# Dense feed-forward: VectorE, ScalarE and SyncE also issue in program order, side work placed step by step between matmul groups, and the last batch's first two weight quarters keep their sums on chip

## The chip, the core and the metric

The kernel runs on one core of a Trainium2 chip. The metric is the device time of one execution in microseconds (us); smaller is better. Besides TensorE (PE; its weight loads are shown as PEld) the profile names VectorE (DVE), ScalarE (ACT), GpSimd (POOL) and SyncE (SP), which here only issues DMA transfers.

## What is computed

Three layers follow one another over 4 batches of 576 positions: decayed causal attention with 8 heads of 64, a feed-forward block, and a second attention with 4 experts of which two are chosen for each position. The change touches the middle one:

```python
def _moe_ref(x, U, V, w_ch1, w_ch2):           # x (4, 576, 512), w_ch1 (512, 2048)
    xt = x.transpose(0, 2, 1)
    h = xt @ U @ V
    u = x + h.transpose(0, 2, 1)
    ch = np.maximum(u @ w_ch1, 0.0) @ w_ch2     # w_ch2 (2048, 512)
    return (u + ch).astype(np.float32)
```

Every factor is split into a high and a low part, and three products (high by high, high by low, low by high) are summed in PSUM.

## The kernel before

**Steps and groups.** The 2048 hidden columns are cut into four quarters, and each batch into two halves c of 288 positions. One step is a batch, a half and a quarter: 32 steps. `ffn_stream` runs them as one generator. Step i alternates four *hidden* groups (`ffn_hidden`, L529, for step i+1: twelve matmuls into PSUM tile `hps`, then `hh` by ACT in L533 and `hl` by DVE in L534) with four *out* groups (`ffn_out`, L545, for step i: twelve matmuls into `cps`, then a DVE addition into `ust` or `yc`, L548 or L550). Both PSUM tiles come from one pool of three buffers, `psf`. Each `yield` of the stream ends one group. In the following such a group and the time it takes on PE is called a **slot**; slot 1 is the first one after the first attention has ended (402.20 us).

**Quarters 0 and 1** work in a 32-bit format (fp32r) with weights that are prepared during the first attention. Steps 0 to 15 use them: batch 3 last, first quarter 0 for both halves (steps 12 and 13), then quarter 1 for both (14 and 15). After quarter 0 its sums go to `ydram`; for quarter 1 `ffn_load` reads `ust` from `udram` again, casts it again to `uh` (L514, ACT) and `ul` (L515, POOL), and reads the sums back (L519). For batches 0 to 2 the sums stay on chip between the two quarters.

**Quarters 2 and 3** work in fp16, with scales. Steps 16 to 23 do quarter 2 and then 3 for batches 0 and 1, steps 24 to 31 for batches 2 and 3. What they need is made as *side work* beside steps 9 to 23:

- `narrow_quarter`: for each of 8 weight pieces a quarter, a 512 KB transfer into `raw` (two buffers), two ACT operations (L338, L340), two DVE operations (L341, L342, here called the joining) and a DVE maximum (L423). The next transfer into a buffer can start when the joining of the piece in it is done.
- `power`: turns a maximum into a scale over a transpose on PE (`amt`, L384), three small DVE operations on `ar` (L388 to L390), a matmul (`rsp`, L395) and two DVE operations.
- `prepare_u`: reads `ust` of a batch (576 KB for each half) and takes four DVE maxima `uam` (L465), then `power`.
- `convert_quarter` and `convert_u`: high part by ACT, low part by DVE (L448, L449 and L488, L489).

**Who orders what.** `dense_until` runs one slot of the stream, then one step of each job. But only PE was held to program order (`manual_schedule`). For DVE, ACT, SP and POOL a scheduler set the order of each queue at build time, from its own estimate of when each instruction can start. On the chip each queue is then worked off in the order that was set: an instruction that waits holds up what stands behind it on its engine.

At the end of the stretch the weights of the third layer (`wall`, `wo`) and the result of batch 0 (`load_y`) are read and split, again at places that the scheduler chose.

Of the kernel before, what the change touches and what calls it, by code (L numbers as in the profile page):

```python
# [18 lines left out]
P = 128  # L19
# [42 lines left out]
def kernel(  # L62
# [271 lines left out]
    def narrow_bytes(wt, raw):  # L334

        lo, hi = raw[:, :, 0], raw[:, :, 1]
        wi = wt.bitcast(I32)
        nc.scalar.activation(wi, raw.bitcast(U8)[:, :, 3], AF.Copy, bias=-31.0 / 64.0,  # L338
                             scale=1.0 / 32.0)
        nc.scalar.activation(f32(lo), f32(hi), AF.Copy, scale=2.0 ** -112)  # L340
        nc.vector.scalar_tensor_tensor(wi, lo, 3, wi, OP.logical_shift_left, OP.bitwise_or)  # L341
        nc.vector.scalar_tensor_tensor(wi, hi, -2147483648, wi, OP.bitwise_and, OP.bitwise_or)  # L342
# [58 lines left out]
    def narrow_quarter(w32, q):  # L401
# [34 lines left out]
    def convert_quarter(w32, q):  # L436

        w1h, w1l, w2h, w2l = W[q]
        sides = scales[q][0]
        for t in range(2 * FT):  # L440
            cs = slice(t * P, t * P + P)
            if t < FT:
                dh, dl = w1h[:, :, cs], w1l[:, :, cs]
                sv = w32[:, t, :].rearrange("p (k n) -> p k n", k=KT)
            else:
                dh, dl, sv = w2h[:, t - FT, :], w2l[:, t - FT, :], w32[:, t, :]
            up = sides[t // FT][:, 1:2]
            nc.scalar.mul(dh, sv, up)  # L448
            nc.vector.scalar_tensor_tensor(dl, sv, up, dh, OP.mult, OP.subtract)  # L449
            yield  # L450
# [23 lines left out]
    def convert_u(b, ycs):  # L474

        us, es = st_u.pop(b)
        uh = cur["fu"].tile([P, KT, S], F16, name="uhf", tag="uh")
        ul = cur["fu"].tile([P, KT, S], F16, name="ulf", tag="ul")
        for c, yc in enumerate(ycs):
            cs = slice(c * HC, c * HC + HC)  # L480
            nc.sync.dma_start(yc[:], ydram[b, :, :, cs])
            for i, step in enumerate(steps):
                if step[:2] == (b, c) and step[2] > 1:
                    loads[i] = uh[:, :, cs], ul[:, :, cs], yc, es
        for c in range(NC):
            cs = slice(c * HC, c * HC + HC)
            for k in range(0, KT, 2):
                nc.scalar.mul(uh[:, k:k + 2, cs], us[c][:, k:k + 2], es[:, 1:2])  # L488
                nc.vector.scalar_tensor_tensor(ul[:, k:k + 2, cs], us[c][:, k:k + 2], es[:, 1:2],  # L489
                                               uh[:, k:k + 2, cs], OP.mult, OP.subtract)  # L490
                yield
# [11 lines left out]
    def ffn_load(b, c, first, fy):  # L503
# [10 lines left out]
        nc.scalar.copy(uh[:], ust[:])  # L514
        nc.gpsimd.tensor_tensor(ul[:], ust[:], f32(uh[:]), OP.subtract)  # L515
        if first:
            return uh, ul, ust
        yc = fy.tile([P, KT, HC], F32, name="yc", tag="yc")
        nc.sync.dma_start(yc[:], ydram[b, :, :, cs])  # L519
        return uh, ul, yc  # L520
# [37 lines left out]
    for q in (0, 1):  # L558
        steps += [(B - 1, c, q, q == 0, True, True) for c in range(NC)]
# [7 lines left out]
    W, loads, scales = {}, {}, {}  # L567

# [9 lines left out]
    def ffn_stream():  # L578
# [8 lines left out]
        for i, (b, c, q, first, head, last) in enumerate(steps):  # L587
# [6 lines left out]
            for j in range(KT):  # L594
                if i + 1 < n:
                    q1 = steps[i + 1][2]
                    nxt.append(ffn_hidden(j, W[q1], *loads[i + 1][:2], F32R if q1 < 2 else F16))
                    yield i
                ffn_out(j, W[q], hs, yc, back)
                late = QX0 <= i + 2 < QX1  # L600
                if j == 1 and not late and (i + 2 > 4 * (B - 1) or (i + 2) % 4):
# [3 lines left out]
                if j == KT - 1 and late:  # L605
                    ffn_prepare(i + 2)
# [375 lines left out]

    more_weights(100)
    with tc.manual_schedule(engines={mybir.EngineType.PE}):
        jobs.append(in_turn(narrow_quarter(w32[2], 2), narrow_quarter(w32[3], 3)))
        jobs.append(in_turn(prepare_u(0, fy2), prepare_u(1, fy2)))
        dense_until(QX0)
        halves_of_weights()
        drain(jobs[1]) if len(jobs) > 1 else None
        del jobs[1:]  # L990
        quarters = [convert_quarter(w32[2], 2)]
        jobs.append(convert_u(0, sums_of(fy2, ("yc", "yc"))))
        while 2 not in scales:
            next(jobs[0])
        jobs.append(in_turn(*quarters))
        dense_until(QX1 - 1)
        jobs.append(convert_u(1, sums_of(fy2, ("yc", "yc"))))
        dense_until(QX1)
        drain(in_turn(*jobs))
        del jobs[:]  # L1000
        jobs.append(convert_quarter(w32[3], 3))
        dense_until(QX1 + 1)
        jobs.append(prepare_u(2, cur["fy"]))
        dense_until(QX1 + 5)
        jobs.append(in_turn(convert_u(2, sums_of(wy_pool, ("w1h", "w1l"))),
                            prepare_u(3, cur["fy"])))
# [3 lines left out]
        jobs.append(convert_u(3, sums_of(wy_pool, ("w2h", "w2l"))))  # L1010
# [16 lines left out]
    for k in range(KT):  # L1027
        for c0, c1 in ((0, 512), (512, NA)):
            st = stage.tile([P, 512], F32, name="st3", tag="wst")
            nc.sync.dma_start(st[:, 0:c1 - c0], wall[k * P:k * P + P, c0:c1])  # L1030
            nc.scalar.copy(wah[:, k, c0:c1], st[:, 0:c1 - c0])
            nc.gpsimd.tensor_tensor(wal[:, k, c0:c1], st[:, 0:c1 - c0], f32(wah[:, k, c0:c1]),
                                    OP.subtract)
    for k in range(2):
        st = stage.tile([P, 512], F32, name="st3b", tag="wst")
        nc.sync.dma_start(st[:], wo[k * P:k * P + P, :])
        nc.scalar.copy(woh[:, k, :], st[:])
        nc.gpsimd.tensor_tensor(wol[:, k, :], st[:], f32(woh[:, k, :]), OP.subtract)
# [7 lines left out]
    def load_y(b, yp, stp, tag):  # L1046
# [3 lines left out]
        nc.gpsimd.memset(f32(yl[:, :, S:SP_]), 0.0)  # L1050
        for c in range(NC):
            cs = slice(c * HC, c * HC + HC)
            st = stp.tile([P, KT, HC], F32, name="yst", tag=tag)
            nc.sync.dma_start(st[:], ydram[b, :, :, cs])
            for k in range(KT):
                nc.scalar.copy(yh[:, k, cs], st[:, k])
                nc.gpsimd.tensor_tensor(yl[:, k, cs], st[:, k], f32(yh[:, k, cs]), OP.subtract)
        return yh, yl

    y = load_y(0, sy0, fy, "yc")  # L1060
    with tc.manual_schedule(engines={mybir.EngineType.PE}):
        dense_until(len(steps))
    for p_ in (s16, fy, fh, fu, wy_pool, wx_pool, stage):
# [245 lines left out]
    with tc.manual_schedule(engines={mybir.EngineType.PE}):  # L1309
# [16 lines left out]
        one(m1)  # L1326
        with tc.issue_after(first_k):
            y_next = load_y(1, ys[1], sy, "yst")
        for h in range(NH):
# [5 lines left out]
            if e == 1 and b + 2 < B:  # L1335
                with tc.issue_after(cur["last"].ins):
                    y_next = load_y(b + 2, ys[b % 2], sy, "yst")
# [89 lines left out]
```

## Time and profile before

| | us |
|---|---|
| median of 3 runs | 894.58 |
| lowest to highest | 893.28 to 894.96 |
| profiled execution, its own time | 901.39 |
| its span from first to last instruction | 899.7 |
| mean granted TensorE clock | 0.964 of full |
| PE / DVE / ACT / POOL busy over the span | 795.6 / 608.0 / 428.8 / 282.8 |

The profiled execution is 6.8 us above the median. Shares of the whole span mix three layers with different limits; the change lies in the stretch from about 402 to 699 us, so that stretch is read by itself in the rows below.

### The profile page before, as it was taken

The page shows a single profiled execution, that of the slowest core. Times are in us where ns is not written, and L with a number is a line of the kernel's source. Part 1 is how long each engine was busy: PE and PEld are TensorE (multiplying, and loading weights), DVE is VectorE, ACT ScalarE, POOL GpSimd, SP SyncE. Part 2 cuts the span into 40 slices and gives each one's busy share as a digit, 9 for nine tenths or more (in the row PEclk, how much of TensorE's full clock was granted, in tenths as well). Part 3 has the DMA queues.
Part 4 walks back from the last instruction along what each step waited for, and adds up shares of the span by engine and source line. Part 5 has one row for each costly group of instructions (what it writes and reads, how often), then busy time and mean ns, then how long its engine had stood idle before and what let it go on. Part 6 is the DMA issues. An engine that isn't in the chain of part 4 may idle for free.

```text
span 899.7 us, 19048 instructions
## 1 busy us (share of the span) xinstructions
PE 795.6 (88%) x7412; PEld 720.2 (80%) x7412; DVE 608.0 (68%) x1598; ACT 428.8 (48%) x840; POOL 282.8 (31%) x367
## 2 busy tenths in 40 slices
PE   2588578899999999989797989999999989989997
PEld 2587477788999889989796867777777989979886
DVE  6889978975777666657778533553333678877775
ACT  3677557555545564334454311223211467665664
POOL 9856554543423442002011000007200635331210
PEclk9988789999999999999989999999999999999999
DMA  6334565543433441155566321321200530312122
GB/s 190 107 108 132 169 205 152 164 131 93 131 113 88 135 122 53 38 184 173 168 199 199 100 97 43 90 80 52 79 28 27 146 87 21 101 47 75 35 77 84
DMA packets 63146, 97.23 MB, mean 108 GB/s; under 512 B 5024, under 2 KB 43792, under 8 KB 63056
## 3 DMA queue, kind: packets, MB, share of 16 engines
q1 hardware_dynamic: 58496, 87.24, 33.1%
q10 hardware_dynamic: 4560, 8.78, 2.7%
q8 instruction: 58, 0.95, 0.5%
q14 instruction: 32, 0.26, 0.1%
HBM read 55.61 MB, written 22.56 MB: 87 GB/s over the span
## 4 chain that ended last, share of the span: by engine, by line
PE 54%; DVE 19%; DMA 14%; ACT 5%; issue 4%; POOL 3%; SPq 1%; POOLq 0%; ACTq 0%; DVEq 0%
PE cps L545 15%; PE hps L529 14%; PE sc L228 6%; DVE ph L244 4%; DMA ust<-udram 4%; DMA raw<-in_w_dram 3%; PE po L1227 3%; PE pv L1185 3%; DVE ub L185 2%; PE pq L1120 2%; PE ub L180 2%; DMA ydram<-ust 2%; PE gp L734 2%; PE av L259 1%; PE av L263 1%
## 5 line engine op out<-in xcount | busy, mean ns | idle before, releaser
L244 DVE TENSOR_TENSOR ph<-pf,ph 128x576 f16<-128x576 f32 x144 | 128.6, 898 | 31.8 <-ACT ph L243 31.1
L533 ACT ACTIVATE hh<-hps 128x288 fp32r<-128x288 f32 (+1 forms) x128 | 52.3, 409 | 203.6 <-PE hps L529 198.2
L534 DVE SCALAR_TENSOR_TENSOR hl<-hps,hh 128x288 fp32r<-128x288 f32 (+1 forms) x128 | 57.9, 453 | 88.8 <-ACT hh L533 88.4
L238 ACT ACTIVATE pf<-sc 128x576 f32<-128x576 f32 x144 | 84.3, 613 | 36.8 <-PE sc L228 32.2
L243 ACT CAST ph<-pf 128x576 f16<-128x576 f32 x144 | 89.7, 638 | 10.1 <-POOL pf L240 8.7
L228 PE MATMUL sc<-qa,ka 128*128 128x288 f32 (+4 forms) x288 | 75.8, 324 | 18.5 <-DMA qa<-mr 6.9
L185 DVE CUSTOM_DVE_ANT_0 ub<-ub,maskm 128x448 f32<-128x448 f32 x192 | 81.8, 426 | 11.5 <-PE ub L180 9.4
L545 PE MATMUL cps<-hh,w2h 128*128 128x288 f32 x256 | 81.2, 317 | 1.2 <-DVE ust L548 0.9
L545 PE MATMUL cps<-hh,w2hf 128*128 128x288 f16 x256 | 73.8, 288 | 7.4 <-DVE hl L534 7.4
L529 PE MATMUL hps<-uh,w1h 128*128 128x288 f32 x256 | 76.3, 319 | 3.7 <-DVE hl L534 2.8
L545 PE MATMUL cps<-hh,w2l 128*128 128x288 f32 x256 | 77.6, 303 | 0.0
L545 PE MATMUL cps<-hl,w2h 128*128 128x288 f32 x256 | 77.5, 303 | 0.1
L259 PE MATMUL av<-vh,ph 128*128 128x65 f16 x720 | 74.7, 199 | 2.0 <-DVE x L308 2.0
L261 PE MATMUL av<-vl,ph 128*128 128x64 f16 x720 | 74.2, 196 | 0.0
L263 PE MATMUL av<-vh,ph 128*128 128x65 f16 x720 | 74.0, 196 | 0.0
L545 PE MATMUL cps<-hl,w2hf 128*128 128x288 f16 x256 | 73.8, 288 | 0.0
L545 PE MATMUL cps<-hh,w2lf 128*128 128x288 f16 x256 | 73.8, 288 | 0.0
L228 PEld LDWEIGHTS sc<-qa,ka 128*128 128x128 f32 x288 | 53.8, 207 | 23.8 <-ACT pf L238 5.5
L259 PEld LDWEIGHTS <-ph 128*128 128x128 f16 x720 | 67.7, 100 | 6.1 <-DVE x L308 2.1
L529 PE MATMUL hps<-uh,w1l 128*128 128x288 f32 x256 | 71.9, 302 | 0.0
L261 PEld LDWEIGHTS <-ph 128*128 128x128 f16 x720 | 68.2, 101 | 0.0
L263 PEld LDWEIGHTS <-ph 128*128 128x128 f16 x720 | 68.1, 100 | 0.0
(222 smaller groups left out, 2377.4 us busy)
## 6 DMA issues: line engine op xcount, KB each, us to landing
raw<-in_w_dram SPq DMA_DIRECT2D x32, 512.0 KB
qkt<-in_qk_dram SPq DMA_DIRECT2D x16, 576.0 KB
ust<-udram SPq DMA_DIRECT2D x16, 576.0 KB
ydram<-yc SPq DMA_DIRECT2D x14, 576.0 KB
yc<-ydram SPq DMA_DIRECT2D x10, 576.0 KB
vr<-in_v_dram SPq DMA_DIRECT2D x16, 320.0 KB
udram<-ustage ACTq DMA_DIRECT2D x16, 288.0 KB
ydram<-ust SPq DMA_DIRECT2D x8, 576.0 KB
```

The costliest lines, as they stand in the source:

```text
L185: nc.vector.tensor_tensor_reduce(ub[:, bk, off:off + w], ub[:, bk, off:off + w], maskm[:, S - w:S], 1.0, NEG, OP.add, OP.max, mx[:, t:t + 1])
L228: nc.tensor.matmul(ps[:, bk, off:off + w], wa, xa, start=bk not in banks[:n], stop=bk not in banks[n + 1:])
L238: nc.scalar.activation(pfv, view, AF.Exp, scale=ISC)
L243: nc.scalar.copy(ph[:, o0:o0 + n], pf[:, 0:n])
L244: nc.vector.tensor_tensor(pl[:, o0:o0 + n], pf[:, 0:n], ph[:, o0:o0 + n], OP.subtract)
L259: nc.tensor.matmul(av[:, it, :], ph[:, c:c + P], vh[:, jt, :], start=first, stop=False)
L261: nc.tensor.matmul(av[:, it, 0:64], ph[:, c:c + P], vl[:, jt, :], start=False, stop=False)
L263: nc.tensor.matmul(av[:, it, :], pl[:, c:c + P], vh[:, jt, :], start=False, stop=last)
L529: nc.tensor.matmul(ph[:], wa[:, k, fs], xa[:, k], start=n == 0, stop=n == 3 * KT - 1)
L533: nc.scalar.activation(hh[:], ph[:], AF.Relu)
L534: nc.vector.scalar_tensor_tensor(hl[:], ph[:], 0.0, hh[:] if dt == F16 else f32(hh[:]), OP.max, OP.subtract)
L545: nc.tensor.matmul(pc[:], wa[:, t, dsl], xa[:], start=n == 0, stop=n == 3 * FT - 1)
```

## The change

1. In the two regions of the dense stretch, DVE, ACT and SP are held to program order as PE was. POOL is still ordered by the scheduler.
2. `narrow_quarter` is cut into steps: the ACT part of a piece in one slot, the joining, the maximum and the next-but-one transfer in the next slot; for quarter 3 (`slow`) the maximum goes into a third slot. The first two transfers are issued ahead.
3. `behind_by_one` gives ACT the high part of one piece and DVE the low part of the piece before it in the same slot, one pair each slot. Quarter 2's pieces and batch 0's input are taken in turns, in slots 38 to 50; batch 1's input follows in slots 54 to 58, quarter 3's pieces after its scales are there (slots 70 to 78).
4. Batch 3 keeps `uh`, `ul` and its sums on chip from quarter 0 to quarter 1: four loads, two stores and two pairs of casts go away. The remaining casts of the stretch are done in two halves, each in a slot of its own (`cast_some`).
5. The loads of the sums for batches 2 and 3 and the maxima of their inputs, and the weights of the third layer, are placed in slots too; one part of these weights is cast every other slot.

The matmuls are the same, in the same order except for `amt` and `rsp`, which stand between other groups. Outside the stretch the queues are the same.

```diff
+    def low_bits(wt, raw):
+        lo, hi = raw[:, :, 0], raw[:, :, 1]
+        nc.scalar.activation(wt.bitcast(I32), raw.bitcast(U8)[:, :, 3], AF.Copy, bias=-31.0 / 64.0,
+                             scale=1.0 / 32.0)
+        nc.scalar.activation(f32(lo), f32(hi), AF.Copy, scale=2.0 ** -112)
...
         read(0)
+        yield
+        read(1)
+        yield
         for t in range(2 * FT):
-            if t + 1 < 2 * FT:
-                read(t + 1)
+            words = raws[t][:].rearrange("p (n two) -> p n two", two=2)
+            low_bits(w32[:, t, :], words)
             yield
-            narrow_bytes(w32[:, t, :], raws.pop(0)[:].rearrange("p (n two) -> p n two", two=2))
-            yield
+            join_bits(w32[:, t, :], words)
+            if slow:
+                yield
             nc.vector.tensor_reduce(am[:, t // FT, t % FT:t % FT + 1], w32[:, t, :], AX.X, OP.max,
                                     apply_absolute_value=True)
+            if t + 2 < 2 * FT:
+                read(t + 2)
+            yield
...
+    def behind_by_one(pairs):
+        last = None
+        for high, low in pairs:
+            high()
+            if last:
+                last()
+            last = low
+            yield
+        last()
+        yield
...
+    def cast_some():
+        if casts:
+            dh, dl, sv = casts.pop(0)
+            nc.scalar.copy(dh, sv)
+            nc.gpsimd.tensor_tensor(dl, sv, f32(dh), OP.subtract)
...
     for q in (0, 1):
-        steps += [(B - 1, c, q, q == 0, True, True) for c in range(NC)]
+        steps += [(B - 1, c, q, True, q == 0, q == 1) for c in range(NC)]
...
+    IN_ORDER = {mybir.EngineType.PE, mybir.EngineType.DVE, mybir.EngineType.Activation,
+                mybir.EngineType.SP}
     more_weights(100)
-    with tc.manual_schedule(engines={mybir.EngineType.PE}):
-        jobs.append(in_turn(narrow_quarter(w32[2], 2), narrow_quarter(w32[3], 3)))
+    dense.append(True)
+    with tc.manual_schedule(engines=IN_ORDER):
+        jobs.append(in_turn(narrow_quarter(w32[2], 2, False), narrow_quarter(w32[3], 3, True)))
         jobs.append(in_turn(prepare_u(0, fy2), prepare_u(1, fy2)))
         dense_until(QX0)
...
+        begin_u(0, sums_of(fy2, ("yc", "yc")))
+        jobs.append(behind_by_one(convert_u(0, (0,)) + convert_w(w32[2], 2, EARLY)
+                                  + convert_u(0, (1,)) + convert_w(w32[2], 2, LATE)))
         dense_until(QX1 - 1)
-        jobs.append(convert_u(1, sums_of(fy2, ("yc", "yc"))))
+        begin_u(1, sums_of(fy2, ("yc", "yc")))
         dense_until(QX1)
+        jobs.append(behind_by_one(convert_u(1)))
+        dense_until(QX1 + 1)
+        jobs.append(prepare_u(2, cur["fy"]))
+        while 3 not in scales:
+            dense_until(at[0] + 1)
+        jobs.append(behind_by_one(convert_w(w32[3], 3, (*EARLY, *LATE))))
...
+        for n, (src, dh, dl, w) in enumerate(parts):
+            nc.scalar.copy(dh, sts[n][:, 0:w])
+            nc.gpsimd.tensor_tensor(dl, sts[n][:, 0:w], f32(dh), OP.subtract)
+            yield
+            yield
+            read(n + 2)
```

**VectorE at the start of the stretch, slots 3 to 8.** `uam` are the maxima of the inputs, `w<-raw` the joining, `wam` the maximum of a weight piece, `ust<-cps` and `hl` the evictions of an out and a hidden group. Before:

```order
L465 TENSOR_REDUCE uam<-ust 128x1 x2
L548 TENSOR_TENSOR ust<-cps,ust 128x288
L465 TENSOR_REDUCE uam<-ust 128x1 x2
L534 SCALAR_TENSOR_TENSOR hl<-hps,hh 128x288
L469 TENSOR_REDUCE ua_6152<-uam 128x1
L548 TENSOR_TENSOR ust<-cps,ust 128x288
L534 SCALAR_TENSOR_TENSOR hl<-hps,hh 128x288
L548 TENSOR_TENSOR ust<-cps,ust 128x288
L341 SCALAR_TENSOR_TENSOR w_5790<-raw,w_5790 128x512 x2
```

The same place in the changed kernel:

```order
L584 TENSOR_TENSOR ust<-cps,ust 128x288
L486 TENSOR_REDUCE uam<-ust 128x1
L570 SCALAR_TENSOR_TENSOR hl<-hps,hh 128x288
L345 SCALAR_TENSOR_TENSOR w_5790<-raw,w_5790 128x512
L346 SCALAR_TENSOR_TENSOR w_5790<-raw,w_5790 128x512
L431 TENSOR_REDUCE wam<-w_5790 128x1
L486 TENSOR_REDUCE uam<-ust 128x1
L584 TENSOR_TENSOR ust<-cps,ust 128x288
L486 TENSOR_REDUCE uam<-ust 128x1
L570 SCALAR_TENSOR_TENSOR hl<-hps,hh 128x288
L345 SCALAR_TENSOR_TENSOR w_5790<-raw,w_5790 128x512
L346 SCALAR_TENSOR_TENSOR w_5790<-raw,w_5790 128x512
```

The eight input maxima of batches 0 and 1 no longer stand together ahead of the first piece; they stand one in a slot, beside the joinings, batch 0's in slots 3 to 6 and batch 1's in slots 13 to 16.

**SyncE's queue from step 15's end to the inputs of batch 2.** `ust<-udram` is the input that the maxima read, `ydram<-yc` a store of finished sums, `yc<-ydram` a load of sums. Before:

```order
L604 DMA ydram<-yc 512x1x288
L459 DMA ust<-udram 128x4x288
L481 DMA yc<-ydram 128x4x288
L604 DMA ydram<-yc 512x1x288
L459 DMA ust<-udram 128x4x288
L481 DMA yc<-ydram 128x4x288
```

The same place in the changed kernel:

```order
L644 DMA ydram<-ust 512x1x288
L644 DMA ydram<-yc 512x1x288
L480 DMA ust<-udram 128x4x288 x2
L644 DMA ydram<-yc 512x1x288 x4
L501 DMA yc<-ydram 128x4x288 x2
```

Both loads of batch 2's input now stand behind the first store of step 16, in buffers of which none is still being stored.

## Rows read from the trace of the kernel before

**Rows 1.** Stretches: start:end, length; PE, PEld, DVE, ACT, POOL busy; clock, DMA share, GB/s.

```profile
402.00:434.00 32.00, 31.22 (x234) 30.56 (x232) 24.71 (x51) 14.93 (x27) 5.70 (x2) 1.00 0.55 170
...
526.00:616.00 90.00, 90.00 (x738) 71.77 (x736) 39.32 (x90) 21.09 (x49) 3.77 (x11) 1.00 0.23 73
```

**Rows 2.** Waits of PE, 402 to 700 us: total us, times, longest.

```profile
PE cps L545 <- DVE hl L534: 7.7, 5, 4.0
PE rsp L395 <- DVE ar L390: 6.2, 2, 3.5
PE amt L384 <- DVE ar L388: 2.6, 1, 2.6
PE hps L529 <- POOL ul L515: 1.4, 1, 1.4
PE hps L529 <- ACT uh L514: 0.9, 1, 0.9
PE cps L545 <- DVE ust L548: 0.9, 1, 0.9
PE hps L529 <- DVE hl L534: 0.4, 1, 0.4
```

**Rows 3.** Chain of waits in order of time: start us, us, what; groups of matmuls.

```profile
402.36 1.60 PE cps L545 x12
...
449.80 3.09 PE hps L529 x12
452.89 2.88 PE cps L545 x12
...
492.53 2.10 PE hps L529 x12
494.63 2.56 PE cps L545 x12
...
521.01 3.04 PE cps L545 x12
...
550.67 1.47 PE hps L529 x12
...
698.93 3.19 PE pq L1120 x24
```

**Rows 4.** TensorE timeline just ahead of slot 1.

```profile
401.50 0.38 PE L744 MATMUL up<-vs,g 128*128 128x256 f32 x1 [1.32 <-DVE g L736]
402.20 0.29 PE L545 MATMUL cps<-hh,w2h 128*128 128x288 f32 x1
```

**Rows 5.** Chain of waits again: the transfers on it.

```profile
414.98 6.21 DMA raw<-in_w_dram
...
427.92 3.65 DMA raw<-in_w_dram
...
507.37 7.47 DMA ydram<-yc
...
514.86 4.30 DMA ust<-udram
```

**Rows 6.** Timelines, ScalarE then VectorE: one piece's first operations, then two evictions.

```profile
421.21 0.67 ACT L338 ACTIVATE w<-raw 128x512 int32<-128x512 uint8 x1 [2.37 <-DMA raw<-in_w_dram]
...
422.62 0.69 DVE L341 SCALAR_TENSOR_TENSOR w<-raw,w 128x512 int32<-128x512 int32 x1 [1.45 <-ACT raw L340]
...
424.67 0.45 DVE L534 SCALAR_TENSOR_TENSOR hl<-hps,hh 128x288 fp32r<-128x288 f32 x1
425.04 0.45 DVE L548 TENSOR_TENSOR ust<-cps,ust 128x288 f32<-128x288 f32 x1
```

**Rows 7.** VectorE groups by line and shape, 398 to 705 us: busy us, mean ns, idle.

```profile
L489 DVE SCALAR_TENSOR_TENSOR ulf<-ust,es,uhf 128x576 f16<-128x576 f32 x16 | 14.3, 920 | 5.9 <-ACT uhf L488 5.9
...
L465 DVE TENSOR_REDUCE uam<-ust 128x1 f32<-128x576 f32 x16 | 11.3, 746 | 10.5 <-DMA ust<-udram 10.5
...
L449 DVE SCALAR_TENSOR_TENSOR w1lf<-w,es,w1hf 128x512 f16<-128x512 f32 x8 | 5.8, 740 | 0.2 <-ACT w1hf L448 0.2
```

More of the change, by code (lines that the diff above doesn't have):

```diff
@@ L513, in ffn_load @@
         ul = fu.tile([P, KT, HC], F32R, name="ul", tag="ul")
[L514 to L520, printed above, removed]
+        if dense:
+            for k in range(0, KT, 2):
+                casts.append((uh[:, k:k + 2], ul[:, k:k + 2], ust[:, k:k + 2]))
+        else:
+            nc.scalar.copy(uh[:], ust[:])
+            nc.gpsimd.tensor_tensor(ul[:], ust[:], f32(uh[:]), OP.subtract)
+        return uh, ul, ust
+    def cast_some():
[3 more added lines that the diff above has]
+            nc.gpsimd.tensor_tensor(dl, sv, f32(dh), OP.subtract)
     def ffn_hidden(t, weights, uh, ul, dt=F32R):
@@ L567 @@
     W, loads, scales = {}, {}, {}
+    dense, casts = [], []
     def ffn_prepare(i):
@@ L1026, with second_weights, read @@
     wol = sw.tile([P, 2, DM], F32R, name="wol")
[L1027 to L1038, printed above, removed]
+    def second_weights():
+        parts = [(wall[k * P:k * P + P, c0:c1], wah[:, k, c0:c1], wal[:, k, c0:c1], c1 - c0)
+                 for k in range(KT) for c0, c1 in ((0, 512), (512, NA))]
+        parts += [(wo[k * P:k * P + P, :], woh[:, k, :], wol[:, k, :], DM) for k in range(2)]
+        sts = []
+        def read(n):
+            if n < len(parts):
+                src, dh, dl, w = parts[n]
+                sts.append(stage.tile([P, 512], F32, name="st3", tag="wst"))
+                nc.sync.dma_start(sts[n][:, 0:w], src)
+        read(0)
+        yield
+        read(1)
+        yield
+        yield
+        for n, (src, dh, dl, w) in enumerate(parts):
+            nc.scalar.copy(dh, sts[n][:, 0:w])
+            nc.gpsimd.tensor_tensor(dl, sts[n][:, 0:w], f32(dh), OP.subtract)
+            yield
+            yield
+            read(n + 2)
     tie = sw.tile([P, E, E], F32, name="tie")
@@ L1050, in load_y @@
         nc.gpsimd.memset(f32(yl[:, :, S:SP_]), 0.0)
+        out += yh, yl
+        sts = [stp.tile([P, KT, HC], F32, name="yst", tag=tag) for c in range(NC)]
+        for c in range(NC):
+            nc.sync.dma_start(sts[c][:], ydram[b, :, :, c * HC:c * HC + HC])
+        yield
+        yield
         for c in range(NC):
             cs = slice(c * HC, c * HC + HC)
-            st = stp.tile([P, KT, HC], F32, name="yst", tag=tag)
-            nc.sync.dma_start(st[:], ydram[b, :, :, cs])
             for k in range(KT):
[L1056 to L1061, printed above, removed]
+                nc.scalar.copy(yh[:, k, cs], sts[c][:, k])
+                nc.gpsimd.tensor_tensor(yl[:, k, cs], sts[c][:, k], f32(yh[:, k, cs]), OP.subtract)
+                yield
+    y = []
+    with tc.manual_schedule(engines=IN_ORDER):
+        jobs.append(in_turn(second_weights(), load_y(0, sy0, fy, "yc", y)))
         dense_until(len(steps))
+        drain(in_turn(*jobs))
     for p_ in (s16, fy, fh, fu, wy_pool, wx_pool, stage):
```

93 lines of the change are left out of this document (46 added, 47 removed).

## Prediction

> **What bounds the kernel now.** I read the stretches first, then PE's waits, then the chain of waits in order of time. From 526 to 616 us PE is busy in every microsecond at full clock while DVE and ACT are below half [rows 1]: there the dense layer runs at PE's own pace, and nothing on another engine can help it. So the question is how far the rest of the stretch is from that pace. PE's own pace is read from undisturbed groups on the chain: 1.60 us for a slot of quarters 0 and 1, 1.47 us for one of quarters 2 and 3 [rows 3]. From slot 1 at 402.20 [rows 4] to the first matmul of the next layer at 698.93 [rows 3] are 296.7 us. The program has 49 slots of the first kind left at that point (27 out, 22 hidden) and 128 of the second: 49 x 1.60 + 128 x 1.47 = 266.6, and some 1.6 for the small matmuls between them, an estimate of 0.2 for each of eight pairs. That is 268.2, so **28.5 us are lost** to something other than PE's work.
>
> PE's waits name most of it: 7.7 + 6.2 + 2.6 + 1.4 + 0.9 + 0.9 + 0.4 = 20.1 us [rows 2]. Behind three of the waits the next groups took nearly twice their time: 3.09 and 2.88 against 1.60, 2.10 against 1.47 and 2.56 against 1.60, 3.04 against 1.47 [rows 3]; that is 1.49 + 1.28 + 0.63 + 0.96 + 1.57 = 5.9 us at a lower granted clock. The last 2.5 us are gaps too small to be named. One more wait stands just ahead: 1.32 us until DVE's `g` [rows 4], which came late because maxima of the inputs stood in front of it.
>
> **The change part by part.**
>
> *What goes away.* PE waited for DVE (`hl`, `ar`) or for the reloaded batch 3 (`uh`, `ul`), and each time DVE's queue held something else first. (1) The two `rsp` waits and the `amt` wait, 8.8 us: DVE finished `ar` late since a joining that waited for its transfer, or low parts of batch 1's input, stood between the three `ar` operations. In the changed order these three stand together, and the matmul that needs them comes two slots later. (2) The wait of 4.0 for `hl`: its eviction stood behind maxima whose `ust` landed late, because the load had to wait for a store of 7.47 us out of the same buffer and then took 4.30 itself [rows 5]. Now both loads go to free buffers. (3) `ul`, `uh` and `ust` around the reload, 1.4 + 0.9 + 0.9: batch 3's second quarter loads and casts nothing. (4) The other 3.7 us in four `hl` waits lie mostly at the weights of the third layer, where `hh` stood behind casts that waited for their transfer; now one part is cast every other slot, and its transfer is issued as soon as its buffer is free, two slots or more ahead. So all 28.5 are open, and of the 1.32 for `g` about 0.9, as `g` now stands ahead of the maxima.
>
> *What comes new.* A queue in program order makes PE wait wherever DVE's work in a few slots exceeds them. The slack is set by the three PSUM buffers: the eviction of a slot must be done before the third slot after it, so it may be late by two slots less itself, 3.2 - 0.5 = 2.7 us.
>
> (a) Slots 3 to 19. DVE has 17 evictions of about 0.40 (0.45 long, 0.37 apart [rows 6]), 6.8; eight pieces at 2.05 (422.62 to 424.67 [rows 6]), 16.4; eight maxima of 0.75 [rows 7], 6.0; small operations 1.5. Sum 30.7 us for 17 x 1.60 = 27.2. The excess is 3.5, and an estimated 1.6 more, one slot, comes from the work being bunched at the end: about 5.1 late at slot 17, less 2.7 of slack, **2.4 us of PE's time if every transfer lands in time**. But the transfers form a loop: a buffer is free when its joining ends, the issue takes about 0.4, the transfer 3.65 alone or 6.21 with another one in the queue [rows 5], ACT 1.4 (421.21 to 422.62), the joining another 1.4, two thirds of the 2.05 [rows 6]. That is 6.8 to 9.4 us, and each buffer has four slots, 6.4. Six pieces are read in this window, three rounds of the loop; about half have company (a store, batch 1's input, batch 3's). The upper bound is 3 x (9.4 - 6.4) - 2.7 = 6.3. I walked slot by slot, with 3.65 for lone transfers and 6.21 for those in company, counting from the end of slot 3. DVE begins the eviction of slot 9 at 12.4 (due 9.7, as soon as PE is done), of slot 11 at 16.9 (due 12.9), of slot 15 at 24.9 (due 19.3), of slot 17 at 29.3 (due 22.5): 6.8 late, less 2.7 of slack, and PE loses **4.1 us**. The late transfers and DVE's own excess partly cover each other; this value lies between the ends and uses both rows, so I take it. Behind a late transfer ACT's queue holds `hh` of the next hidden group, and PE waits for that. The kernel before did the same work in 402 to 434 us with 0.8 us of idle [rows 1], since the input maxima ran ahead.
> The Trainium skill (DMA: Bandwidth & Descriptors, section Anatomy of one DMA — SWDGE (gpsimd) path) gives for a transfer issued by GpSimd 2.0 us plus bytes over 436 GB/s: an estimate of 3.2 us for these 0.52 MB, by which the loop would take 6.4 us, fit its four slots, and leave only the 2.4, a time 1.7 us shorter than forecast. The rows of 3.65 and 6.21 are longer, and I go by them.
>
> (b) Slots 38 to 50: 13 evictions 5.2, four low parts of the input at 0.92 [rows 7] 3.7, eight of the weights at 0.74 [rows 7] 5.9, four pieces at 2.05 and one maximum more 8.9, in all 23.7 against 10 x 1.60 + 3 x 1.47 = 20.4. 3.3 late against 2.7 of slack: I take **0.7**. Bounds 0 and 2.6: the last piece of quarter 3 queues behind a store and two loads, and company costs 6.21 - 3.65.
> (c) Batch 2's maxima in slots 64 to 67: the load is issued behind the store of step 16, some 1.4 us after slot 61 has ended, and takes 6.2 in company; DVE is there 4.9 us after that end, waits 2.7, and has about that slack. **0.2**, bounds 0 and, with 7.47 for the transfer [rows 5], 1.3.
> (d) The end: casts every other slot, ACT well below its slots. **0.2**, bounds 0 and one of the old waits there, 0.9.
> (e) Of the 2.5 in small gaps half stays: **1.2**, bounds 0 and 2.5.
>
> *Sum.* New losses 4.1 + 0.7 + 0.2 + 0.2 + 1.2 = 6.4, bounds 2.4 and 13.6. The profiled execution would take 901.4 - 28.5 - 0.9 + 6.4 = 878.4 us. It lay 6.8 above the median of the runs, so the median becomes **871.6**, with 867.6 to 878.8 from the bounds. PE is busy without a break up to the next layer, and the queues after it are unchanged, so the whole gain reaches the end.
>
> **The rivals.**
> *The waits gather (883).* If late transfers bunch PE's small waits in (a) into two gaps like those before 449.64 and 521.01, and (b) into one, the clock falls behind each: (a) 6.3 + 2 x 2.8, (b) 2.6 + 1.6, the rest 1.6, in all 17.7 against 6.4. For it: both `rsp` waits and the 4.0 were followed by slow groups [rows 2, 3]. Against: the `amt` wait of 2.6 and the three waits of 0.9 to 1.4 at the reload were not.
> *Everything hides (868).* Transfers land alone, (a) is 2.4 and the rest near 0: 28.5 + 0.9 - 2.9 less. For it: the same transfers took 3.65 where nothing else ran.
> *Slower (897).* The loop of (a) sets the pace: program order ties ACT's evictions to the transfers, as each joining and each `hh` now stands behind the piece before it. With transfers of 14 us the loop takes 17.2, three rounds lose 3 x (17.2 - 6.4) - 2.7 = 29.7, and with the other 2.3 that is 2.6 more than the 29.4 saved. It decides from about 13 us for each transfer, twice the 6.21; the longest on the chain, a store, took 7.47 [rows 5].
> *It does not do what it says (894).* The gaps only move: each wait of the old order is replaced by one of the new, as the transfers and DVE's work are nearly the same in sum. Against: where nothing waits DVE is busy 39.32 of 90 us [rows 1], so there is room to place the work; only slots 3 to 19 and 38 to 50 are tight.
>
> **How the numbers follow.** Forecast 0.61, waits gather 0.17, everything hides 0.12, slower 0.05, gaps only move 0.05. The first three are faster, 0.90; the last gives 0.04 within 0.2% (1.8 us, about what a measurement of this kernel can tell from no change) and 0.01 slower, so slower has 0.06. The range, 866 to 884, takes in the first three.
>
> **What would show it.** In the changed profile PE should go without a named wait of over 1 us from about slot 20 to the next layer, except near slots 40 to 52; the groups behind `rsp` should take 1.47 to 1.60; batch 3's reloads should be gone; and ACT's waits for `raw` should sit in the first 30 us, with PE idle there 3 to 6 us where before it was 0.8. I am wrong if PE idles much longer in that window, if the clock falls in it, or if the next layer starts later than 680 us into the span.

## The result, and the profile after

| measurement | changed, median (lowest to highest, runs) | before, median (runs) | ratio, 95% interval |
|---|---|---|---|
| first | 883.64 (878.40 to 884.62, 4) | 894.77 (4) | 0.9861, 0.9814 to 0.9907 |
| second | 877.25 (874.67 to 880.14, 6) | 897.88 (11) | 0.9768, 0.9737 to 0.9800 |
| third | 879.88 (871.59 to 885.08, 6) | 898.20 (11) | 0.9789, 0.9720 to 0.9858 |

The change makes the kernel faster. The first measurement, for which the prediction was made, gives 11.1 us; the forecast was 871.6, a gain of 23, with 866 to 884 as the range, so the median lies 0.4 us inside its upper end. The two intervals at the top do not overlap, so measurements differ by more than the runs inside one of them. Over all five measurements of this study the median of the kernel before is 895.8 (66 runs), that of the changed kernel over its three 879.3 (16 runs): **16.5 us**. Six of the 66 runs and two of the 16 were in a slower state of the chip; the ratios leave them out, and without them the medians are 895.6 and 879.1, again 16.5 us apart.

What is steadier than the time of a run is the stretch that was changed: from slot 1 to the first matmul of the next layer (`pq`), both read from TensorE's timeline.

| kernel | slot 1 | next layer | stretch | behind it |
|---|---|---|---|---|
| before, first profile | 402.2 | 698.7 | 296.5 | 201.0 |
| before, second profile | 395.3 | 688.6 | 293.2 | 201.7 |
| changed, first profile | 400.1 | 680.6 | 280.6 | 200.4 |
| changed, second profile | 398.2 | 676.5 | 278.2 | 201.2 |
| changed, third profile | 398.1 | 678.0 | 279.9 | 200.8 |

Means 294.9 and 279.6: 15.3 us less, and 0.9 more for the wait on `g` just ahead (1.32 in [rows 4], 0.45 now). That is 16.2 us, which agrees with the 16.5 of the medians. The forecast was 22.1 and 0.9. From profile to profile of one kernel the stretch differs by 3.3 us (before) and 2.4 us (changed). Each variant below has a single profile, so a difference of that size says little, and what is read is which gaps come and go.

First the stretches of the changed kernel (columns as in [rows 1]):

```profile
402.00:434.00 32.00, 28.77 (x193) 27.89 (x191) 23.53 (x44) 11.89 (x21) 2.69 (x1) 0.89 0.52 161
434.00:448.00 14.00, 10.09 (x74) 9.67 (x75) 12.35 (x27) 4.87 (x10) 3.26 (x2) 1.00 0.33 109
448.00:598.00 150.00, 150.00 (x1202) 127.71 (x1201) 92.05 (x207) 50.81 (x98) 1.39 (x6) 1.00 0.36 117
598.00:628.00 30.00, 28.40 (x232) 22.50 (x231) 9.07 (x22) 7.99 (x19) 15.31 (x23) 1.00 0.38 115
```

From 448 to 598 us PE is busy in every microsecond at full clock. The time that is left to win lies in the first 46 us and in one gap behind 598. TensorE's waits from 402 to 690 us, to be held against [rows 2]:

```profile
PE hps L565 <- DVE ust L584: 4.1, 2, 2.8
PE rsp L399 <- DVE ar L394: 2.2, 1, 2.2
PE cps L581 <- DVE hl L570: 1.8, 2, 1.6
PE amt L388 <- DVE ua L490: 0.7, 1, 0.7
```

The 20.1 us have become 8.8. The chain of waits shows the groups behind the longest one, at 414.22 (2.84 us):

```profile
414.22 3.25 PE hps L565 x12
417.46 2.88 PE cps L581 x12
420.50 1.60 PE hps L565 x12
```

Two groups took 3.25 and 2.88 against 1.60, 2.9 us more. The granted clock there was 0.50, the lower of its two levels (1.2 GHz):

```profile
415.00:418.00 3.00, 3.00 (x15) 3.00 (x14) 2.93 (x6) 1.72 (x3) 0.00 (x0) 0.50 0.84 271
```

What DVE did ahead of that gap stands in two timelines, GpSimd's and then VectorE's:

```profile
408.46 2.69 POOL L548 TENSOR_TENSOR ul<-ust,uh 128x1152 fp32r<-128x1152 f32 x1 [30.72 <-ACT uh L547]
...
439.30 3.26 POOL L556 TENSOR_TENSOR ul<-ust,uh 128x576 fp32r<-128x576 f32 x2 [28.15 <-ACT uh L555]
```

```profile
408.72 0.46 DVE L570 SCALAR_TENSOR_TENSOR hl<-hps,hh 128x288 fp32r<-128x288 f32 x1 [2.56 <-ACT hh L569]
409.09 2.60 DVE L345 SCALAR_TENSOR_TENSOR w<-raw,w 128x512 int32<-128x512 int32 x1
411.73 0.69 DVE L346 SCALAR_TENSOR_TENSOR w<-raw,w 128x512 int32<-128x512 int32 x1
...
439.38 1.89 DVE L345 SCALAR_TENSOR_TENSOR w<-raw,w 128x512 int32<-128x512 int32 x1
441.31 1.80 DVE L346 SCALAR_TENSOR_TENSOR w<-raw,w 128x512 int32<-128x512 int32 x1
```

An operation of a joining (it has two), elsewhere 0.68 or 0.69 us, takes 2.60, 1.89 and 1.80 us just where GpSimd subtracts `ul`. The first of them ends 0.54 us after GpSimd's operation (411.69 and 411.15). The eviction `hl`, which reads PSUM and one SBUF tile, takes its usual 0.46 beside the same subtraction. The same stands in the timelines of the kernel before, GpSimd's and VectorE's:

```profile
423.70 2.88 POOL L515 TENSOR_TENSOR ul<-ust,uh 128x1152 fp32r<-128x1152 f32 x1 [7.38 <-ACT uh L514]
```

```profile
425.46 1.66 DVE L341 SCALAR_TENSOR_TENSOR w<-raw,w 128x512 int32<-128x512 int32 x1
```

Here too the joining's operation ends 0.54 us behind the subtraction (427.12 and 426.58), while the maximum `wam` at 424.07, with one SBUF input, took its usual 0.69 beside it. That became the theory of the experiments: **GpSimd's subtraction holds VectorE's operations with two SBUF inputs** (SBUF is the on-chip memory of all tiles but the PSUM ones). The rival was the one of the prediction's term (a): the loop of transfers and DVE's own load set these 46 us.

Something else stood ahead of the first gap too. DVE came late to the joining, since it had waited 2.56 us for `hh`, and ScalarE's timeline shows why:

```profile
407.22 1.16 ACT L547 CAST uh<-ust 128x1152 fp32r<-128x1152 f32 x1 [2.09 <-DMA ust<-udram]
408.29 0.40 ACT L569 ACTIVATE hh<-hps 128x288 fp32r<-128x288 f32 x1
```

The cast of batch 3's first half waited for its load, and `hh` stood behind it. It is a whole one of 1152 columns: the casts in halves of part 4 of the change begin only with batch 3's second half.

### The profile page after: what moved, and what is told of

It is laid out like the page before. It is cut to its first block, busy times and chain, and to the rows that moved or that the text cites. A ratio compares the mean times of both kernels' runs of the same rounds, so it can differ in the third digit from the quotient of the medians.

```text
span 881.0 us, 19011 instructions
## 1 busy us (share of the span) xinstructions
PE 787.4 (89%) x7412; PEld 714.1 (81%) x7412; DVE 609.2 (69%) x1598; ACT 426.7 (48%) x839; POOL 277.6 (32%) x366
## 4 chain that ended last, share of the span: by engine, by line
PE 62%; DVE 19%; DMA 9%; issue 3%; ACT 3%; POOL 2%; SPq 1%; POOLq 0%; DVEq 0%; ACTq 0%
PE cps L581 18%; PE hps L565 18%; PE sc L228 7%; DVE ph L244 4%; PE pv L1253 3%; PE po L1295 3%; DMA ust<-udram 3%; DVE ub L185 2%; PE pq L1188 2%; PE ub L180 2%; DMA raw<-in_w_dram 2%; PE gp L772 2%; PE av L259 1%; PE av L263 1%; PE av L261 1%
## 5 line engine op out<-in xcount | busy, mean ns | idle before, releaser
L259 PE MATMUL av<-vh,ph 128*128 128x65 f16 x720 | 72.8, 197 | 2.0 <-DVE x L308 2.0
L261 PE MATMUL av<-vl,ph 128*128 128x64 f16 x720 | 72.3, 195 | 0.0
L263 PE MATMUL av<-vh,ph 128*128 128x65 f16 x720 | 72.1, 195 | 0.0
L259 PEld LDWEIGHTS <-ph 128*128 128x128 f16 x720 | 66.5, 98 | 6.1 <-DVE x L308 2.1
L228 PE MATMUL sc<-qb,kb 128*128 128x288 f32 (+4 forms) x288 | 68.5, 321 | 0.0
L261 PEld LDWEIGHTS <-ph 128*128 128x128 f16 x720 | 67.1, 100 | 0.0
```

The costliest lines, as they stand in the source:

```text
L228: nc.tensor.matmul(ps[:, bk, off:off + w], wa, xa, start=bk not in banks[:n], stop=bk not in banks[n + 1:])
L259: nc.tensor.matmul(av[:, it, :], ph[:, c:c + P], vh[:, jt, :], start=first, stop=False)
L261: nc.tensor.matmul(av[:, it, 0:64], ph[:, c:c + P], vl[:, jt, :], start=False, stop=False)
L263: nc.tensor.matmul(av[:, it, :], pl[:, c:c + P], vh[:, jt, :], start=False, stop=last)
```

## The experiments

Kernels of one measurement share the runs of the kernel before; all ratios are to it.

**Without GpSimd's subtraction.**

```diff
+            if b == B - 1:
+                nc.gpsimd.memset(f32(ul[:]), 0.0)
...
-            nc.gpsimd.tensor_tensor(dl, sv, f32(dh), OP.subtract)
+            nc.gpsimd.memset(f32(dl), 0.0)
```

> GpSimd's subtraction for batch 3's low part is left out: ul is filled with zeros instead, so this part of the result is missing. Nothing else moves. Theory (GpSimd's subtraction holds DVE's operations with two SBUF inputs): the joinings that took 2.60, 1.89 and 1.80 us return to 0.68, the gaps of PE near 414 and 445 us go (2.8 and 2.2), and with the first one the half clock behind it (2.9); slot 1 to the next layer takes 273 to 276 us instead of 280.8, the run 5 to 8 us less than the changed kernel. Rival (the transfer loop of the weight pieces and DVE's own load set the window): joinings may shorten but both gaps stay within 1 us of their size, the stretch takes 279 to 281, the run the same within 2 us.

VectorE's timeline at the same place, and then its groups by line from 398 to 690 us, first of the changed kernel, then of this one:

```profile
407.44 0.46 DVE L573 SCALAR_TENSOR_TENSOR hl<-hps,hh 128x288 fp32r<-128x288 f32 x1 [2.92 <-ACT hh L572]
407.81 0.68 DVE L345 SCALAR_TENSOR_TENSOR w<-raw,w 128x512 int32<-128x512 int32 x1
```

```profile
L345 DVE SCALAR_TENSOR_TENSOR w<-raw,w 128x512 int32<-128x512 int32 x16 | 14.0, 877 | 0.0
L346 DVE SCALAR_TENSOR_TENSOR w<-raw,w 128x512 int32<-128x512 int32 x16 | 12.2, 761 | 0.6
```

```profile
L345 DVE SCALAR_TENSOR_TENSOR w<-raw,w 128x512 int32<-128x512 int32 x16 | 10.9, 681 | 0.0
L346 DVE SCALAR_TENSOR_TENSOR w<-raw,w 128x512 int32<-128x512 int32 x16 | 11.1, 692 | 0.6
```

The mean of a joining's first half falls from 877 to 681 ns, of the second from 761 to 692: with nothing else changed on DVE, the hold is GpSimd's. The gap near 412 shrinks from 2.8 to 1.2 us, and the two slow groups behind it are gone; the cast ahead of `hh` is still there, and DVE waits 2.92 us for it. The wait near 445 is gone as well. But the stretch takes 276.9, not 273 to 276, and the run 875.50 (ratio 0.9755, 0.9716 to 0.9795), no clear difference to the changed kernel. A gap of 2.60 us has come at 429.52: there DVE, now earlier, waited 3.34 us for batch 1's input (2.02 in the changed kernel's first profile). So the theory holds for its two gaps and not for the whole window.

**The subtraction on DVE**, in two halves of 576 columns, batch 3's first half included. The casts of that half move back by four slots with it, so this edit takes away the hold and the cast ahead of `hh` together:

```diff
-        if dense:
+        if dense or b == B - 1:
+            if not dense:
+                casts.extend([None] * 4)
...
-            nc.gpsimd.tensor_tensor(dl, sv, f32(dh), OP.subtract)
+            nc.vector.tensor_tensor(dl, sv, f32(dh), OP.subtract)
```

> The same subtraction on DVE, in halves of 576 columns in slots of their own, batch 3's first half included: four operations of some 0.7 us more on DVE in slots 8 to 25, none on GpSimd. Theory (GpSimd holds DVE): DVE loses 2.8 us and gets back 4.2, the large waits go; stretch 274 to 278, the run 3 to 7 us less than the changed kernel. Rival (DVE's own load is the limit there, 30.7 us for 27.2): the window gets longer by the 2.8 us that DVE has more to do; stretch 281 to 284, the run 1 to 3 us more.

The stretch takes 276.2, inside the theory's 274 to 278, though DVE does four operations of 0.76 us more; the rival's 281 to 284 is out. From slot 1 to 423 us PE has no gap of 0.5 us or more. VectorE's timeline shows that not all of this is GpSimd's doing:

```profile
408.34 0.46 DVE L573 SCALAR_TENSOR_TENSOR hl<-hps,hh 128x288 fp32r<-128x288 f32 x1 [0.92 <-ACT hh L572]
408.71 0.68 DVE L345 SCALAR_TENSOR_TENSOR w<-raw,w 128x512 int32<-128x512 int32 x1
```

DVE waits 0.92 us for `hh` in place of 2.56, 1.6 less, and the joining's operation is 1.9 shorter. With the hold gone 1.2 us of the first gap were left, with both gone none; the cast alone was not taken away. The run, 876.99 (0.9770, 0.9735 to 0.9805), does not show the 3 us: that is below what runs resolve.

**Batch 1's input ten slots later.**

```diff
-        jobs.append(in_turn(prepare_u(0, fy2), prepare_u(1, fy2)))
+        jobs.append(in_turn(prepare_u(0, fy2), empty(10), prepare_u(1, fy2)))
```

> The load of batch 1's input and its maxima ten slots later, behind the pieces of quarter 2. Theory (GpSimd holds DVE): the gap near 414 stays, since neither stands ahead of it; of those from 435 to 445 (1.2, 0.7, 2.2) at most the 1.2 goes; stretch 279 to 281, the run the same within 1.5 us. Rival (bunching of transfers and maxima): without company the pieces' transfers fall from 6 to about 4 us, the three gaps from 435 to 445 go; stretch 276 to 278, the run 3 to 5 us less.

```profile
402.00:434.00 32.00, 29.16 (x207) 28.57 (x206) 25.24 (x48) 13.61 (x25) 2.68 (x1) 0.95 0.48 154
434.00:448.00 14.00, 13.51 (x101) 12.97 (x100) 9.12 (x26) 2.79 (x6) 2.81 (x2) 1.00 0.63 203
```

Here the rival was right: the gaps from 430 to 445 us go (PE 13.51 of 14 us against 10.09; counted from the same slot, the other two profiles of the changed kernel have 12.4 and 10.5), and the stretch takes 275.0, even below the rival's range. The gap of 2.84 us at 411.88 stays, with a joining's operation of 2.59 us ahead of it, as the theory said. What stood between 430 and 440 in the changed kernel shows in its chain and on VectorE:

```profile
424.82 5.92 DMA ust<-udram
```

```profile
430.76 0.75 DVE L486 TENSOR_REDUCE uam<-ust 128x1 f32<-128x576 f32 x1 [2.02 <-DMA ust<-udram]
```

GpSimd's second subtraction did no harm in this run: it met no joining. The same happened in the second profile of the changed kernel, where the joining began first (GpSimd's timeline, then VectorE's):

```profile
438.33 3.23 POOL L556 TENSOR_TENSOR ul<-ust,uh 128x576 fp32r<-128x576 f32 x2 [28.59 <-ACT uh L555]
```

```profile
438.19 0.69 DVE L346 SCALAR_TENSOR_TENSOR w<-raw,w 128x512 int32<-128x512 int32 x1
```

There `rsp` did not wait; in the first and the third profile, where the two met, it waited 2.19 and 1.99 us. So there are **several causes in three places**: near 412 GpSimd's hold and the cast ahead of `hh`; between 430 and 440 batch 1's input, whose load of 5.92 us shares the queue with the raw pieces and whose four maxima fall on the fullest slots; ahead of `rsp` near 445 the hold again, in the executions in which it meets a joining. The run took 875.85 (0.9745, 0.9709 to 0.9781), like the two kernels above not clear of the changed kernel beside it (0.9768).

**Three edits together:** the subtraction on DVE, the later input, and a third one for the gap at 608.63. That gap in the changed kernel:

```profile
607.15 0.62 ACT L1095 CAST wah<-st 128x512 fp32r<-128x512 f32 x1 [5.50 <-DMA st<-in_wall_dram]
```

```profile
608.63 0.28 PE L581 MATMUL cps<-hh,w2hf 128*128 128x288 f16 x1 [1.60 <-DVE hl L570]
```

ScalarE's cast waited 5.50 us for a transfer of 2.58 us. Its buffer had been held: GpSimd, the one queue that the scheduler still ordered, worked off sixteen clearings of tiles (596.54 to 603.3 us) ahead of the `wal` that frees it. The edit puts fourteen of them behind the weights and holds GpSimd to program order too in this region.

```diff
-    fill_heads(heads)
...
-    with tc.manual_schedule(engines=IN_ORDER):
+    with tc.manual_schedule(engines=IN_ORDER | {mybir.EngineType.Pool}):
...
-        jobs.append(in_turn(second_weights(), load_y(0, sy0, fy, "yc", y)))
+        jobs.append(in_turn(second_weights(), late_heads(), load_y(0, sy0, fy, "yc", y)))
```

> The changed kernel with three edits together: batch 3's subtractions on DVE, batch 1's input ten slots later, and the clearing of the third layer's head tiles on GpSimd behind the weights of that layer instead of ahead of them. Theory (two separate causes in the first 45 us, one at 604 us): each edit removes its own gap, so the stretch from slot 1 to the next layer falls from the 275.0 of the later input alone by 2.8 (gap near 412), some 2.5 (half clock behind it) and 1.1 (gap near 604) to 268 to 271; the run takes 4 to 8 us less than the changed kernel. Rival (the waits only gather elsewhere when one is removed): stretch 274 to 277, the run within 3 us of the changed kernel.

PE is busy for all 30 us from 598 to 628, and the gap near 412 is gone. Yet the stretch takes 274.6, the rival's number. TensorE's timeline has two gaps in their place, and VectorE's shows the wait ahead of the second:

```profile
432.93 0.37 PE L568 MATMUL hps<-uh,w1h 128*128 128x288 f32 x1 [2.00 <-DVE ust L587]
...
443.22 0.27 PE L388 MATMUL amt<-ident,wa 128*1 128x128 f32 x1 [1.86 <-DVE wa L440]
```

```profile
441.73 0.75 DVE L486 TENSOR_REDUCE uam<-ust 128x1 f32<-128x576 f32 x1 [4.79 <-DMA ust<-udram]
```

Both stand behind loads that are awaited too early: batch 3's second half (issued 423.3; ScalarE's cast had to wait until 428.9, and DVE for the cast) and batch 1's input (issued 434.9, there at 441.7). The run took 873.87 (0.9787, 0.9743 to 0.9831).

**The same, spread out:** batch 3's second half two slots later and on GpSimd again, batch 1's input looked at three slots later.

```diff
+            casts.extend([None] * (2 if dense else 4))
...
+        jobs.append(in_turn(prepare_u(0, fy2), empty(9), prepare_u(1, fy2, 3)))
```

> The three edits of the last combination, spread out: batch 3's first half is subtracted on DVE in slots 9 and 10, its second half on GpSimd but two slots later (when its load has landed and the joinings are through), batch 1's input is read where the combination read it but looked at three slots later, the heads are cleared late. Theory (the two gaps of 2.0 and 1.9 us that were left stand behind loads of 5.6 and 6.8 us that were awaited too early): both go, stretch 268 to 272 instead of 274.6, the run 1.5 to 6 us less than that combination. Rival (DVE's own load in the window is the limit, so a gap goes only to come back): stretch 273.5 to 276, the run within 2 us of that combination.

```profile
402.00:434.00 32.00, 30.40 (x221) 28.97 (x220) 27.64 (x55) 14.65 (x27) 1.46 (x2) 1.00 0.57 182
434.00:448.00 14.00, 13.26 (x100) 12.80 (x100) 7.50 (x24) 1.65 (x4) 1.33 (x1) 1.00 0.40 120
448.00:598.00 150.00, 150.00 (x1209) 125.64 (x1208) 92.30 (x205) 52.82 (x103) 4.80 (x7) 1.00 0.35 114
598.00:628.00 30.00, 30.00 (x247) 23.96 (x246) 10.69 (x24) 8.07 (x20) 15.65 (x27) 1.00 0.29 90
```

271.8, as the theory said, 6.4 to 8.8 us below the three profiles of the changed kernel; PE is idle for 2.3 us from 402 to 448 and loses no clock. Counted from the same slot (398.4 to 430.4 us here), DVE is busy for 25.7 of 32 us, against 23.53 in the changed kernel, so its own load was not what limited that one. The run took 871.95 (0.9733, 0.9679 to 0.9788): faster than the kernel before, while the interval overlaps those of the second and third measurement of the changed kernel, and only the profiles tell the two apart.

**Which part of the change carries the gain?** Four kernels. The on-chip line alone, in the kernel before:

```diff
-        steps += [(B - 1, c, q, q == 0, True, True) for c in range(NC)]
+        steps += [(B - 1, c, q, True, q == 0, q == 1) for c in range(NC)]
```

> The kernel before with one line of the change: batch 3's first two quarters keep uh, ul and the sums on chip. Theory (it removes its own three waits, 3.2 us): stretch 292 to 295 instead of 296.5, the run 1 to 4 us less than the kernel before. Rival (four loads and two stores less also make the other transfers earlier, so the waits of 4.0 and 3.5 shrink too): stretch 284 to 290, the run 6 to 12 us less.

The stretch takes 289.8, just inside the rival's range and 3.4 to 6.7 us below the profiles of before; the run 890.50 (0.9939, 0.9909 to 0.9969), 4.6 us less, between the two. The waits at the reload are gone, and `rsp`, 6.2 in [rows 2] and 3.0 in the second profile of before, waits for 1.8; `hl` waits eleven times, for 11.4 us.

The change without the order on DVE, ACT and SP:

```diff
-    IN_ORDER = {mybir.EngineType.PE, mybir.EngineType.DVE, mybir.EngineType.Activation,
-                mybir.EngineType.SP}
+    IN_ORDER = {mybir.EngineType.PE}
```

> The changed kernel with only TensorE held to program order; DVE, ACT and SP are ordered by the scheduler again, the code in steps stays. Theory (the order is what removes the waits): the input maxima stand ahead of the joinings and evictions again, waits of 2 to 4 us for hl and ar come back, stretch 285 to 293, the run 6 to 13 us more than the changed kernel. Rival (the steps and the shorter reload alone do it): stretch 277 to 282, the run within 3 us.

```profile
PE cps L581 <- DVE hl L570: 10.0, 6, 4.3
PE rsp L399 <- DVE ar L394: 5.9, 3, 4.5
PE cps L581 <- DVE ua L490: 2.9, 1, 2.9
```

Nothing of the gain is left: 295.8 for the stretch, 894.82 for the run (1.0002, 0.9974 to 1.0030), more than the theory had expected, and worse than the on-chip line alone. The old waits are back; at 495.51 DVE holds two maxima that had waited 5.16 us for `ust`, with evictions behind them.

DVE's order without ACT's and SP's:

> The changed kernel with TensorE and DVE held to program order, ACT and SP ordered by the scheduler. Theory (DVE's order is the part that counts, since the waits named were for what DVE wrote late): stretch 279 to 284, the run within 4 us of the changed kernel. Rival (ACT's and SP's order count as much: the scheduler puts the transfers and casts where DVE's fixed order then waits for them): stretch 287 to 300, the run 8 us or more above the changed kernel.

281.7 and 878.38 (0.9822, 0.9767 to 0.9877): some 2 us above the mean of the changed kernel's stretches, about what these differ by, and 14 below the one with PE's order alone. **With the steps and the on-chip sums in place, DVE's order carries nearly all of it.**

And the order alone, put on the old code:

> The kernel before with DVE, ACT and SP held to program order in the two regions of the dense stretch, its code otherwise as it was. Theory (order without steps is worse than the scheduler): the old code issues all of a job's step at one place and whole blocks at the region's borders, so evictions stand behind transfers; stretch 300 to 320, the run 4 to 24 us more than the kernel before. Rival (order alone brings most of the gain): stretch 278 to 288, the run 8 to 18 us less.

309.6 and 914.40 (1.0218, 1.0174 to 1.0262), slower as the theory said. TensorE's longest wait, and ScalarE ahead of it:

```profile
PE hps L529 <- ACT uh L514: 17.6, 2, 8.8
```

```profile
466.50 1.15 ACT L514 CAST uh<-ust 128x1152 fp32r<-128x1152 f32 x1 [7.41 <-DMA ust<-udram]
```

In program order the cast of a reload stands at the head of ScalarE's queue until its load lands. On the old code as it is, the order costs more than it brings. But both waits of 8.8 us stand at batch 3's reloads, which part 4 of the change takes away, and without these 17.6 us the stretch would be about 292, an estimate that leaves the clock behind the gaps as it is. Order on the old code with the sums kept on chip was not run, nor DVE's order alone on it, so how much of the gain needs the steps themselves is not shown.

**The two kernels once more.** For the time and the spread of the stretch:

> The changed kernel once more, as the measure for the other kernels of this call. Theory (the old profile alone was a slow execution): the profiled execution lies within 2 us of the median of the runs, and the ratio to the kernel before stays at 0.985 to 0.990, about 11 us. Rival (a profiled execution always takes some 7 us more): the profile of this one lies 5 to 8 us above its median.

> The kernel before once more, for a second profile of it. Theory (the stretch itself is steady, what varies from run to run lies ahead of and behind it): slot 1 to the next layer takes 295 to 298 us as in the first profile (296.5), while slot 1 starts anywhere from 394 to 403. Rival (the waits in the stretch vary from run to run by as much): it differs by 4 us or more.

> The changed kernel a third time. The first call gave a ratio of 0.9861 to the kernel before, the second 0.9768. Theory (the stretch is steady, the two differ by what lies outside it): slot 1 to the next layer takes 278 to 281 us again, and the ratio falls between the two, 0.977 to 0.986. Rival (the second value was the exception): the ratio is 0.985 or more.

The changed kernel's profiles lay at +2.1 and +0.7 us to their medians, that of before at -1.5 in its second measurement (893.45 in the median, ratio to the runs beside it 0.9985, 0.9944 to 1.0026): the 6.8 us of the first profile belonged to that one execution. The ratio of 0.985 to 0.990 that was expected of the second measurement did not come; it gave 0.9768, and the third, 0.9789, lies between the first two, as expected. The second stretch of before was 293.2, 3.3 us shorter than the first: below the theory's 295 to 298 and short of the rival's 4 us. Part of the 6.8 thus lay inside the stretch.

## Why the prediction was right, and where it was not

The sign, the place and the mechanism held; the forecast gain was too large, and the first measurement lies in the range with little to spare.

- **What bounds the kernel.** Right: 150 us without a gap from 448 to 598. PE's own work of 268.2 us fits as well, since the variant that is spread out comes within 3.6 us of it.
- **What goes away.** Mostly right. Of (1), 8.8 us, 2.9 are left in the first profile (2.2 before `rsp`, 0.7 before `amt`, both just behind the slots of (a)). (2), the 4.0 behind the `ust` of batch 2, is gone. (3) is gone, and alone it gives 4.6 us in the medians (2.8 to 8.1 by the interval of the ratio), which fits its 3.2. The cause, that something else stood first in DVE's queue, is what the experiments on the order show.
- **The size of what was lost.** 28.5 us came from one profile, and the 6.8 us by which it lay above the median were subtracted as if they lay elsewhere. Its 296.7 also ran to a row at 698.93, where the timeline has the first `pq` at 698.68. The mean of two profiles is 294.9 - 268.2 = 26.7. That is 1.8 of the miss.
- **Term (a): this is the step that failed.** It had 4.1 us for slots 3 to 19. By TensorE's timeline these slots took 8.7, 8.6 and 8.5 us more than 17 x 1.60 in the three profiles of the changed kernel (403.25 to 439.18 us in the first; some 0.4 of it the small matmuls), about twice the term. With the slots next to them, from 402 to 448 us, PE lost 3.23 + 3.91 of idle time and 2.9 by the clock in the first profile, 10.0 us. The walk used about 0.68 us for a joining's operation wherever it stood, and GpSimd's column was left out; yet the trace of before had one of 1.66 us at 425.46 beside a subtraction at 423.70 (2.88). It named a late transfer that holds `hh` in ScalarE's queue, but for the raw pieces; in the first gap it was batch 3's first half. It also gave batch 1's input no place of its own: the maxima were counted, but not that all four wait for one load of 5.92 us in the fullest slots. Where all three are mended, 2.3 us of idle time are left. That is close to the 2.4 that the prediction gave for transfers that land in time, in part by luck, since batch 1's maxima then lie behind these slots.
- **Terms (b), (c), (d), (e).** (b) and (c), 0.7 (its 3.3 less 2.7 is 0.6) and 0.2, were nothing. (d), 0.2, was 1.6: transfers and casts were weighed there, not GpSimd's queue, which the change left to the scheduler. (e), 1.2, was some 0.7.
- **The sum.** New losses 12.4, 10.0 and 11.7 in the three profiles, 11.4 in the mean, for 6.4. With the 1.8 above that is 6.8 us, which is the difference between 23.0 and 16.2. The remaining 5 us between these 16 and the 11.1 of the first measurement are its own; what differed in it is not known.
- **The rivals.** *Waits gather (883)* came out as the time of the first measurement, by luck: the stretch in that profile was 15.9 us shorter than before, not 11. Half its mechanism came: small waits did bunch in (a), with slow groups behind one gap, but (b) did not. *Everything hides (868)* is what the last variant nears. *Slower* did not occur: raw transfers on the chains took 3.5 to 6.2 us, far from 13. *Only moved gaps* is the fate of the change without the order on DVE, ACT and SP.
- **What would show it.** By its own marks the prediction failed in three, in the first profile: waits of over 1 us at 444.78 and 608.63, a clock below full in the window, and a next layer at 680.6 instead of before 680.
- **The rule on the DMA time.** The Trainium skill (DMA: Bandwidth & Descriptors, section Anatomy of one DMA — SWDGE (gpsimd) path) gave an estimate of 3.2 us for a raw transfer, by its formula for transfers that GpSimd issues; here SyncE issues them. The 3.52 and 3.67 of lone transfers in the chain of the spread-out variant lie 0.3 to 0.5 above; those in company, up to 6.2 us, are not covered.

The rule that mattered was another. The Trainium skill (SBUF — State Buffer, section Summary: rules for kernel authors) says that where DVE has two SBUF inputs while a GpSimd operation reads SBUF, the second one to issue "fully blocks until the first finishes". The traces agree: the joining's operations of 2.60 and 1.66 us began 0.63 and 1.76 us behind GpSimd's operation and ended 0.54 us behind its end.

## What to carry to other kernels

Where an engine off the critical path shares something with one that is on it, its operations belong in the slot-by-slot sum at the place where they fall, not in an average; look in the trace of before for the same instruction with two durations. An order written by hand can lose where an operation is not placed behind the landing of its data (here 17.6 us at two casts), and the queue that decides it may be a single one (here VectorE's). Take the loss of a stretch from two profiles if there are two, and compare variants by the stretch rather than by the whole run.

## What was not expected of the hardware

A gap of PE of nearly the same length was followed by a lower granted clock in some profiles and not in others. Behind 2.84 us (changed, first profile) it was at the lower of its two levels for two groups; behind 2.98 us at the same place in the third profile it stayed at the full 2.4 GHz:

```profile
412.40 0.40 PE L565 MATMUL hps<-uh,w1h 128*128 128x288 f32 x1 [2.98 <-DVE ust L584]
```

```profile
414.00:417.00 3.00, 2.29 (x18) 2.05 (x18) 2.96 (x7) 1.65 (x3) 0.00 (x0) 1.00 0.77 231
```

Behind 3.13 us in the second profile the mean was 0.60 from 414 to 417 us, and behind 2.60 us at 429.52 in the kernel without the subtraction 0.56 from 431 to 434. So the length of one gap does not decide it here, and a forecast can only give the loss behind a gap (2.9 and 1.6 us in the first two profiles) a chance. What decides it was not tested.
